# Rows of the second pair of sequences: turned by VectorE in squares of 32 and stored by SyncE, four tiles at a time

## Chip, cores and metric

The kernel runs on one core of a Trainium2 chip. The metric is the time of one execution on the device in microseconds (us). Engines are named as in the profile: PE is TensorE (PEld its weight loads), DVE VectorE, ACT ScalarE, POOL GpSimd, SP SyncE.

## What is computed

Sliding-window attention with a linear bias by distance for 8 sequences of 576 positions and 8 heads of 64, followed by a mixture of 8 experts in which each token goes to its best expert only.

```python
scores = q @ k.T / sqrt(64)                       # per sequence and head
scores = where(0 <= i - j < 128, scores - slope[h] * (i - j), -1e9)
attn = softmax(scores) @ v                        # (8, 8, 576, 64)
x = attn.transpose(0, 2, 1, 3).reshape(4608, 512)
logits = x @ w_gate                               # (4608, 8)
e = argmax(logits, 1); gate = softmax(logits)[e]
y[n] = gate[n] * (relu(x[n] @ w1[e[n]]) @ w2[e[n]])   # w1 512x1024, w2 1024x512
```

All of it is in float32.

## The kernel before

**Attention.** The sequences are taken in four pairs (bp = 0 to 3), the heads in four pairs (hp), which gives 16 units u = 4 bp + hp. A unit has four steps (g = 0 to 3), so the main loop runs over i = 4u + g, from 0 to 63. At each step `scores` are computed some three steps ahead (TensorE at L785, exponentials on ScalarE at L794 and L804, the factor of distance on VectorE at L798), `values` multiplies the probabilities with v into one accumulator (L828), and `finish` closes half a unit: ScalarE copies the accumulator into xT of the pair (L845, L847), TensorE adds up the probabilities (L859) and VectorE or ScalarE put the sums into sumT. There are two xT buffers, so that pair 2 writes into the buffer of pair 0, and pair 3 into that of pair 1. The accumulator `at` has one buffer, the small PSUM tile `m` two.

**Loads.** SyncE loads q, k and v of unit u + 2 during unit u. Each load follows a tiny transfer (`no_earlier_than`, L638) that reads a probability just made and so holds SyncE's queue to the pace of the loop. SyncE works through its queue in order.

**What is done with a finished pair.** `behind(bp)` gives a list of tasks; one is carried out at each step of the pair that follows. They compute the gate logits of the pair (`gate`, `turn`), the softmax scales `es` (`scale_a` to `scale_c`), each token's place (`count`, `place`, `ones_at`, `enlist`), and they write the pair's rows of x, with their scales, to `x_rows` in DRAM. A pair has nine tiles t of 128 rows; the ninth holds the last 64 rows of both sequences. The rows are written in one of two ways:

- *Turned by TensorE* (`row_turned`, `row_out`; pairs 1 and 2): four transposes of 128x128 into PSUM (L1067), a ScalarE copy to a row buffer `xs` (L1069), a POOL copy of the scales (L1076), one store of whole rows of 2,112 bytes by POOL (L1081).
- *Turned by VectorE* (`squares_turned`, `squares_scaled`, `squares_out`; pairs 0 and 3): VectorE transposes the tile in squares of 32 x 32 (L1118), POOL adds the scales brought into the same order (L1126; four small matmuls and two ScalarE copies in `scales_squared` make them once for each pair), and the stores put each square's rows of 528 bytes in their place (L1137): four stores for a tile, eight for the ninth. Pair 3 stores four tiles at a time by SyncE, out of a buffer of its own.

The row buffers come from the pool `rows`, which has four. They go round: a tile that asks for a buffer gets the one used four tiles earlier, and its writer waits until the stores out of it have landed.

**Order.** The order of instructions on each engine is that in which the program issues them (`manual_schedule`); waits for data and for buffers are added to it. After the attention the experts are computed, two after each other with a fast matrix multiplication of seven products. The rows of the first expert are gathered by POOL from `x_rows` of pairs 0 to 2 (L1271) before pair 3 is done; TensorE turns them (L1296) and the experts' matmuls follow.

Of the kernel before, what the change touches and what calls it, by code (L numbers as in the profile page):

```python
# [8 lines left out]
F32 = mybir.dt.float32  # L9
# [7 lines left out]
P = 128  # L17
# [441 lines left out]
def kernel(  # L459
# [12 lines left out]
    nc = tc.nc  # L472
# [12 lines left out]
    TPB = 2 * S // P  # L485
# [13 lines left out]
    NA = P // TQ  # L499
    PD = HP * TQ  # L500
    PW = PD + HP
# [5 lines left out]
    with ExitStack() as fast:  # L507
        def pool(stack, name, bufs, **kw):
            return stack.enter_context(tc.tile_pool(name=name, bufs=bufs, **kw))

        tail, att, late = ExitStack(), ExitStack(), ExitStack()
# [5 lines left out]
        ps_m = pool(fast, "ps_m", 2, space=PSUM)  # L517
        xp = pool(tail, "xp", 2, side="right")
        small = pool(tail, "small", 1, side="right")
        rows = pool(tail, "rows", 4, side="right")  # L520

# [185 lines left out]
        def placed(bp, t):  # L709

            b = 2 * bp * S
            if t < 8:
                return [(0, P, b + t // 4 * S + t % 4 * P)]
            return [(0, KB, b + 4 * P), (KB, KB, b + S + 4 * P)]
# [158 lines left out]
        def gate(bp, c):  # L873
            if bp not in gs:
                gs[bp] = xp.tile([P, 2 * S], F32, name="gs", bufs=1)
            ps = ps_m.tile([P, 512], F32, name="m")
            c0, n = ((0, LQ), (LQ, LQ), (2 * LQ, P))[c]
            for hp in range(HP):
                nc.tensor.matmul(
                    ps[32 * hp : 32 * hp + 32, :n], lhsT=wgd[:, hp, :], rhs=xT[bp][:, hp, c0 : c0 + n],  # L880
                    start=True, stop=True,
                )
            if c < 2:
                nc.vector.tensor_tensor(gs[bp][:, c0 : c0 + n], ps[:, :n], sumT[bp][:, :LQ], op=ALU.add)
            else:
                nc.vector.tensor_tensor(
                    gs[bp][:, c0 : c0 + n].rearrange("p (b q) -> p b q", b=2),
                    ps[:, :n].rearrange("p (b q) -> p b q", b=2),
                    sumT[bp][:, None, LQ:].to_broadcast([P, 2, S - LQ]), op=ALU.add,
                )  # L890
# [5 lines left out]
        def turn(bp, part):  # L896

            if part == 0:
                gsr[bp] = small.tile([P, TPB, P], F32, name="gsr")
            t0, n = ((0, 4), (4, 4), (8, 1))[part]  # L900
            ps = ps_m.tile([P, 512], F32, name="m")
            for k in range(n):
                nc.tensor.transpose(ps[:, k * P : (k + 1) * P], gs[bp][:, (t0 + k) * P : (t0 + k + 1) * P], ident[:])
            nc.scalar.copy(gsr[bp][:, t0 : t0 + n, :].rearrange("p t c -> p (t c)"), ps[:, : n * P])
# [155 lines left out]
            nc.vector.scalar_tensor_tensor(to, in0=sl(0), scalar=64.0, in1=sl(1), op0=ALU.mult, op1=ALU.add)  # L1060

        xs_of = {}

        def row_turned(bp, t):
            ps = ps_m.tile([P, 512], F32, name="m")
            for hp in range(HP):
                nc.tensor.transpose(ps[:, hp * P : (hp + 1) * P], xT[bp][:, hp, t * P : (t + 1) * P], ident[:])  # L1067
            xs = xs_of[bp, t] = rows.tile([P, NA, PW], F32, name="xs")
            nc.scalar.copy(  # L1069
                xs[:, :, :PD].rearrange("p a (h f) -> p h a f", h=HP), ps.rearrange("p (h a f) -> p h a f", h=HP, a=NA),  # L1070
            )
# [11 lines left out]
        def row(bp, t):  # L1083
            row_turned(bp, t)
            row_out(bp, t)
# [3 lines left out]
        spare = {}  # L1089
# [16 lines left out]
        def squares(bp, t):  # L1106
            if (bp, t) not in xs_of:
                if bp in spare and t < TPB - 1:
                    w = NA * PW
                    flat = spare[bp].rearrange("p h n -> p (h n)")  # L1110
                    xs_of[bp, t] = flat[:, t * w : (t + 1) * w].rearrange("p (k w) -> p k w", k=NA)
                else:
                    xs_of[bp, t] = rows.tile([P, NA, PW], F32, name="xs")
            return xs_of[bp, t]

        def squares_turned(bp, t):
            xs = squares(bp, t)
            nc.vector.transpose(  # L1118
                xs[:, :, :PD].rearrange("p k (h j) -> p k h j", h=HP),
                xT[bp][:, :, t * P : (t + 1) * P].rearrange("p h (k i) -> p k h i", k=NA),  # L1120
            )

        def squares_scaled(bp, t, n=1):

            for k in range(t, t + n):
                nc.gpsimd.tensor_copy(squares(bp, k)[:, :, PD:], sq_of[bp][:, k])  # L1126

        def squares_out(bp, t, eng, n=1):
            if n == 1:
                xs = xs_of.pop((bp, t))  # L1130
            else:
                w = NA * PW
                flat = spare[bp].rearrange("p h n -> p (h n)")
                xs = flat[:, t * w : (t + n) * w].rearrange("p (k w) -> p k w", k=n * NA)
            for p0, m, r0 in placed(bp, t):
                for a in range(NA):
                    eng.dma_start(  # L1137
                        x_d[r0 : r0 + n * m, a * PW : (a + 1) * PW].rearrange("(k i) w -> i k w", i=TQ),
                        xs[a * TQ : (a + 1) * TQ, p0 // TQ : p0 // TQ + n * m // TQ, :],
                    )  # L1140
# [120 lines left out]
        def gather(g, src):  # L1261
            nm = "" if g["n"] == NJ else "1"
            g["xg"] = g["pool"].tile([P, g["n"], NA, PW], F32, name="xg" + nm)
            for j in range(g["n"]):
                c = g["c0"] + j
                if in_rows(g):
                    todo = [(g["xg"][:, j].rearrange("p a w -> p (a w)"), src, g_idx[:, c : c + 1])]
                else:
                    todo = [(g["xg"][:, j, k, :], x_pieces, p_idx[:, c - NR * NJ, k : k + 1]) for k in range(NA)]
                for to, where, idx in todo:  # L1270
                    nc.gpsimd.indirect_dma_start(  # L1271
                        out=to, out_offset=None, in_=where, in_offset=bass.IndirectOffsetOnAxis(ap=idx, axis=0),
                    )
# [66 lines left out]
        def behind(bp):  # L1340

            g3 = [lambda k=k: gate(bp, k) for k in range(3)]
            t3 = [lambda k=k: turn(bp, k) for k in range(3)]
            rs = [lambda t=t: row(bp, t) for t in range(TPB)]
            a, a2, b, b2, c, n, q, p, p2, o, o2, e = (
                [lambda f=f: f(bp)] for f in (
                    scale_a, scale_a2, scale_b, scale_b2, scale_c, count, scales_squared, place, place2, ones_at,
                    ones_at2, enlist,
                )
            )  # L1350
            if bp == 0:
                rt = [lambda t=t: squares_turned(bp, t) for t in range(TPB)]
                ro = [
                    lambda t=t: (squares_scaled(bp, t), squares_out(bp, t, nc.gpsimd)) for t in range(TPB)
                ]
                return [g3[0:1], g3[1:2], g3[2:] + t3[0:1], t3[1:], a, a2 + rt[0:1], b + rt[1:2], b2 + rt[2:3],
                        c + n + rt[3:4], [], q + p, p2 + ro[0:4], o, o2, rt[4:6], e + rt[6:8] + ro[4:8]]
            rt, ro = ([lambda t=t, f=f: f(bp, t) for t in range(TPB)] for f in (row_turned, row_out))
            if bp == 1:
                last = [lambda: squares_turned(0, TPB - 1), lambda: squares_scaled(0, TPB - 1),  # L1360
                        lambda: squares_out(0, TPB - 1, nc.gpsimd)]
                return [g3[0:1] + last, g3[1:2], g3[2:] + t3[0:1], t3[1:], a + rt[0:1], a2 + rt[1:2], b + rt[2:3],
                        b2 + rt[3:4], c + n, [], p + ro[0:2], p2 + ro[2:4] + rs[4:5], o + rs[5:6], o2 + rs[6:7], rs[7:8], e + rs[8:9]]
            return [g3, t3, a + a2, b + b2 + rt[0:1], c + n + rt[1:2], rt[2:4], p + p2 + ro[0:4], o + o2 + rs[4:6],
                    rs[6:9] + [early_holes], e + [early_table, lambda: gather(fixed[0], x_d[: 3 * 2 * S, :])]]

        tasks = []
# [20 lines left out]
        for i in range(NG):  # L1388
            u, g = divmod(i, 4)
            bp, hp = units[u]  # L1390
# [34 lines left out]
            if g == 3 and hp == HP - 1 and bp < BP - 1:  # L1425
                tasks.extend(behind(bp))
# [318 lines left out]
```

## Time and profile before

| | us |
|---|---|
| median of 3 runs | 726.83 (726.69 to 732.29) |
| the profiled execution | 679.21 |
| its span, first to last instruction | 677.5 |
| PE busy | 649.8 (96%) |
| DVE busy | 363.9 (54%) |
| ACT busy | 217.0 (32%) |
| POOL busy | 240.3 (35%) |

The span is that of the profiled execution, from its first to its last instruction; the median is that of executions without a profile. Durations and times of day below are in microseconds from the start of the profiled span. In the lists of the profile a line begins with the line of the kernel and the engine; "idle before" is time in which the engine had nothing to run just before that instruction, with what ended it behind the arrow. The attention part takes the first 170 us or so, the experts the rest.

### The profile page before, as it was taken

The page shows a single profiled execution, that of the slowest core. Times are in us where ns is not written, and L with a number is a line of the kernel's source. Part 1 is how long each engine was busy: PE and PEld are TensorE (multiplying, and loading weights), DVE is VectorE, ACT ScalarE, POOL GpSimd, SP SyncE. Part 2 cuts the span into 40 slices and gives each one's busy share as a digit, 9 for nine tenths or more (in the row PEclk, how much of TensorE's full clock was granted, in tenths as well). Part 3 has the DMA queues.
Part 4 walks back from the last instruction along what each step waited for, and adds up shares of the span by engine and source line. Part 5 has one row for each costly group of instructions (what it writes and reads, how often), then busy time and mean ns, then how long its engine had stood idle before and what let it go on. Part 6 is the DMA issues. An engine that isn't in the chain of part 4 may idle for free.

```text
span 677.5 us, 14654 instructions
## 1 busy us (share of the span) xinstructions
PE 649.8 (96%) x6004; PEld 543.5 (80%) x6004; DVE 363.9 (54%) x727; ACT 217.0 (32%) x493; POOL 240.3 (35%) x372
## 2 busy tenths in 40 slices
PE   6899789999999999999999999999999999999995
PEld 5778668787788888978888887889788878878893
DVE  3346748776597768435642761484257426623510
ACT  6767547686331231023102311320231023113200
POOL 8000571325032572247026621732371256112020
PEclk9999989999999999999999999999999999999998
DMA  9887976964438944582376518444823674184010
GB/s 263 238 222 194 313 205 216 321 191 141 145 73 269 328 150 141 177 288 62 127 255 225 166 48 288 165 153 147 304 65 137 219 250 145 58 288 153 1 63 8
DMA packets 63166, 122.00 MB, mean 180 GB/s; under 512 B 5905, under 2 KB 29489, under 8 KB 63090
## 3 DMA queue, kind: packets, MB, share of 16 engines
q1 hardware_dynamic: 51138, 92.51, 42.8%
q0 software_dynamic: 10800, 27.58, 12.9%
q8 instruction: 49, 0.80, 0.5%
q10 hardware_dynamic: 1152, 0.88, 0.4%
q14 instruction: 27, 0.22, 0.1%
HBM read 101.79 MB, written 19.96 MB: 180 GB/s over the span
## 4 chain that ended last, share of the span: by engine, by line
PE 57%; issue 25%; POOL 10%; DMA 4%; DVE 2%; ACT 1%; POOLq 0%; DVEq 0%; ACTq 0%
PE pair1a L1552 4%; PE pair1b L1552 4%; PE pair0b L1495 4%; PE pair0a L1495 4%; PE pair0a L1552 4%; PE pair0b L1552 4%; PE pair2b L1495 4%; PE pair2a L1495 4%; POOL xg L1271 4%; DMA x_rows<-xs 3%; PE pair1b L1495 3%; PE pair1a L1495 3%; PE pair2a L1552 3%; PE pair2b L1552 3%; PE pair0a L1607 2%
## 5 line engine op out<-in xcount | busy, mean ns | idle before, releaser
L1271 POOL DMA_INDIRECT xg<-x_rows,p_idx x124 | 125.4, 1011 | 37.8 <-issue 37.5
L1575 POOL DMA_INDIRECT out_dram<-zo,s_idx x39 | 44.5, 1140 | 244.5 <-DVE zo L1566 142.8
L798 DVE TENSOR_TENSOR pe<-pe,fac 128x512 f32<-128x512 f32 x64 | 43.8, 687 | 45.7 <-ACT pe L794 44.9
L785 PE MATMUL sp<-q_sb,k_sb 64*64 64x192 f32 (+2 forms) x1152 | 58.9, 324 | 6.9 <-DMA q_sb<-in_qT_dram 5.4
L828 PE MATMUL at<-pe,v_sb 64*64 64x192 f32 (+2 forms) x1408 | 58.5, 286 | 3.3 <-issue 3.3
L785 PEld LDWEIGHTS sp<-q_sb,k_sb 64*64 64x64 f32 x1152 | 41.4, 138 | 16.1 <-DMA q_sb<-in_qT_dram 4.4
L828 PEld LDWEIGHTS at<-pe,v_sb 64*64 64x64 f32 x1408 | 47.0, 135 | 9.0 <-issue 6.4
L794 ACT ACTIVATE pe<-sp 128x512 f32<-128x512 f32 x64 | 38.2, 598 | 37.9 <-issue 15.9
L804 ACT ACTIVATE pe<-sp,mid 128x128 f32<-128x128 f32 x128 | 39.7, 366 | 0.0
L1506 ACT ACTIVATE h<-h 128x512 f32<-128x512 f32 x32 | 20.2, 631 | 38.6 <-DVE h L1505 38.6
L859 PE MATMUL m<-pe,ind 128*32 128x192 f32 (+2 forms) x704 | 29.7, 286 | 2.7 <-issue 2.7
L1137 POOL DMA_DIRECT2D x_rows<-xs x48 | 26.0, 549 | 9.5 <-DMA x_rows<-xs 4.6
L1283 DVE TENSOR_TENSOR xn<-xg 128x512 f32<-128x512 f32 x39 | 26.3, 677 | 3.5 <-DMA xg<-x_rows,g_idx 3.0
L859 PEld LDWEIGHTS m<-pe,ind 128*32 128x32 f32 x704 | 23.2, 109 | 5.1 <-issue 3.1
L1299 DVE STREAM_TRANSPOSE xgT<-xn 128x512 f32<-128x512 f32 x31 | 22.0, 711 | 1.1
L538 DVE TENSOR_TENSOR w2s<-w 128x512 f32<-128x512 f32 x16 | 10.9, 684 | 20.8 <-DMA w<-in_moe_w_dram 20.8
L1607 PE MATMUL pair2a<-w,h 128*128 128x512 f32 x48 | 21.1, 592 | 0.0
L1126 POOL COPY xs<-sq 128x16 f32<-128x16 f32 x10 | 2.4, 242 | 52.6 <-ACT sq L1104 52.6
L845 ACT COPY xT<-at 128x640 f32<-128x640 f32 (+1 forms) x32 | 19.0, 594 | 4.5 <-PE at L828 2.6
L1495 PE MATMUL pair0a<-xgT,w 128*128 128x256 f32 x72 | 17.1, 380 | 0.7 <-ACT xgT L1297 0.7
L1495 PE MATMUL pair0b<-xgT,w 128*128 128x256 f32 x72 | 17.2, 382 | 0.0
L1552 PE MATMUL pair1a<-w,h 128*128 128x256 f32 x72 | 17.1, 380 | 0.0
(378 smaller groups left out, 1385.0 us busy)
## 6 DMA issues: line engine op xcount, KB each, us to landing
w<-in_moe_w_dram SPq DMA_DIRECT2D x29, 2048.0 KB, 7.9
k_sb<-in_kT_dram SPq DMA_DIRECT2D x15, 576.0 KB, 5.6
q_sb<-in_qT_dram SPq DMA_DIRECT2D x15, 576.0 KB, 6.3
v_sb<-in_v_dram SPq DMA_DIRECT2D x30, 288.0 KB, 4.9
x_rows<-xs POOLq DMA_DIRECT2D x16, 264.0 KB, 4.7
x_rows<-xs POOLq DMA_DIRECT2D x32, 66.0 KB, 5.7
x_rows<-xT SPq DMA_DIRECT2D x8, 264.0 KB, 5.8
w<-in_moe_w_dram SPq DMA_DIRECT2D x4, 512.0 KB, 8.2
```

The lines of the kernel that those rows point to most:

```text
L785: nc.tensor.matmul(by_distance(sp[c * KB : (c + 1) * KB, r, :GC], kb, 0, n), lhsT=k_sb[u][hs, c, kb * KB : (kb + 1) * KB], rhs=q_sb[u][hs, ...
L794: nc.scalar.activation(outer, sp[:, :, :GC].rearrange("p r (j x) -> p r j x", j=3)[:, :, 0:3:2, :], AF.Exp, scale=SCALE,)
L798: nc.vector.tensor_tensor(outer, outer, fac[:, h0 : h0 + 2, : 2 * w].rearrange("p r (j x) -> p r j x", j=2)[:, :, :, : 2 * KB], op=ALU.mult,)
L804: nc.scalar.activation(pe[:, r, inner], sp[:, r, inner], AF.Exp, bias=mid[:, h0 + r : h0 + r + 1], scale=SCALE,)
L828: nc.tensor.matmul(acc[r * D : (r + 1) * D, c, lo - q0 : hi - q0].rearrange("p (j x) -> p j x", x=KB), lhsT=v_sb[u][c * KB : (c + 1) * KB, ...
L859: nc.tensor.matmul(sm[32 * j : 32 * j + 32, lo - q0 : hi - q0].rearrange("p (j x) -> p j x", x=KB), lhsT=none[:] if pe is None else ind[:, ...
L1271: nc.gpsimd.indirect_dma_start(out=to, out_offset=None, in_=where, in_offset=bass.IndirectOffsetOnAxis(ap=idx, axis=0),)
L1283: nc.vector.tensor_tensor(xn[:], x, s.unsqueeze(3).to_broadcast([P, NA, HP, TQ]), op=ALU.mult)
L1495: nc.tensor.matmul(ps[:, f * 256 : (f + 1) * 256], lhsT=left[m][:, d, fb * P : (fb + 1) * P], rhs=right[m][:, d, :], start=(m in (1, 2, 5) ...
L1552: nc.tensor.matmul(ps[:, :256], lhsT=left[m][:, f, c * P : (c + 1) * P], rhs=right[m][:, f, :], start=(m in (1, 2, 5) and f == 0), stop=Tr ...
L1575: ins = nc.gpsimd.indirect_dma_start(out=out[:, :], out_offset=bass.IndirectOffsetOnAxis(ap=s_idx[:, g["c0"] + j : g["c0"] + j + 1], axis= ...
L1607: nc.tensor.matmul(ps[:], lhsT=g["h"][:, fb, :], rhs=g["w2"][:, fb, :], start=(fb == 0), stop=(fb == FB - 1),)
```

## The change

Pair 1 is now turned by VectorE as pair 0 is, and its first eight tiles are stored by SyncE in two batches of four tiles (four stores of 32 x 16 x 132 numbers for each batch). The four row buffers become one tile `rows4` with four slots: tile t uses slot t mod 4, but the ninth tile (t = 8) uses slot 3. That holds for pairs 0, 1 and 2, and for pair 3's ninth tile. Pair 1's ninth tile is turned and stored one pair later, in the second task of pair 2's list, as pair 0's already was in the first task of pair 1's. `scales_squared` is added for pair 1.

```diff
--- before.py
+++ after.py
@@ -517,7 +517,7 @@
         ps_m = pool(fast, "ps_m", 2, space=PSUM)
         xp = pool(tail, "xp", 2, side="right")
         small = pool(tail, "small", 1, side="right")
-        rows = pool(tail, "rows", 4, side="right")
+        rows = pool(tail, "rows", 1, side="right")
 
 
 
@@ -1060,12 +1060,16 @@
             nc.vector.scalar_tensor_tensor(to, in0=sl(0), scalar=64.0, in1=sl(1), op0=ALU.mult, op1=ALU.add)
 
         xs_of = {}
+        rows4 = rows.tile([P, 4, NA, PW], F32, name="rows4")
+
+        def slot_of_row(t):
+            return rows4[:, 3 if t == TPB - 1 else t % 4]
 
         def row_turned(bp, t):
             ps = ps_m.tile([P, 512], F32, name="m")
             for hp in range(HP):
                 nc.tensor.transpose(ps[:, hp * P : (hp + 1) * P], xT[bp][:, hp, t * P : (t + 1) * P], ident[:])
-            xs = xs_of[bp, t] = rows.tile([P, NA, PW], F32, name="xs")
+            xs = xs_of[bp, t] = slot_of_row(t)
             nc.scalar.copy(
                 xs[:, :, :PD].rearrange("p a (h f) -> p h a f", h=HP), ps.rearrange("p (h a f) -> p h a f", h=HP, a=NA),
             )
@@ -1110,7 +1114,7 @@
                     flat = spare[bp].rearrange("p h n -> p (h n)")
                     xs_of[bp, t] = flat[:, t * w : (t + 1) * w].rearrange("p (k w) -> p k w", k=NA)
                 else:
-                    xs_of[bp, t] = rows.tile([P, NA, PW], F32, name="xs")
+                    xs_of[bp, t] = slot_of_row(t)
             return xs_of[bp, t]
 
         def squares_turned(bp, t):
@@ -1129,9 +1133,12 @@
             if n == 1:
                 xs = xs_of.pop((bp, t))
             else:
-                w = NA * PW
-                flat = spare[bp].rearrange("p h n -> p (h n)")
-                xs = flat[:, t * w : (t + n) * w].rearrange("p (k w) -> p k w", k=n * NA)
+                if bp in spare:
+                    w = NA * PW
+                    flat = spare[bp].rearrange("p h n -> p (h n)")
+                    xs = flat[:, t * w : (t + n) * w].rearrange("p (k w) -> p k w", k=n * NA)
+                else:
+                    xs = rows4[:].rearrange("p s k w -> p (s k) w")
             for p0, m, r0 in placed(bp, t):
                 for a in range(NA):
                     eng.dma_start(
@@ -1359,9 +1366,15 @@
             if bp == 1:
                 last = [lambda: squares_turned(0, TPB - 1), lambda: squares_scaled(0, TPB - 1),
                         lambda: squares_out(0, TPB - 1, nc.gpsimd)]
+                rt = [lambda t=t: squares_turned(bp, t) for t in range(TPB)]
+                scaled = [[lambda t=t: squares_scaled(bp, t, 4)] for t in (0, 4)]
+                ro = [[lambda t=t: squares_out(bp, t, nc.sync, 4)] for t in (0, 4)]
                 return [g3[0:1] + last, g3[1:2], g3[2:] + t3[0:1], t3[1:], a + rt[0:1], a2 + rt[1:2], b + rt[2:3],
-                        b2 + rt[3:4], c + n, [], p + ro[0:2], p2 + ro[2:4] + rs[4:5], o + rs[5:6], o2 + rs[6:7], rs[7:8], e + rs[8:9]]
-            return [g3, t3, a + a2, b + b2 + rt[0:1], c + n + rt[1:2], rt[2:4], p + p2 + ro[0:4], o + o2 + rs[4:6],
+                        b2 + rt[3:4], c + n, [], q + p + scaled[0], p2 + ro[0], o, o2, rt[4:6],
+                        e + rt[6:8] + scaled[1] + ro[1]]
+            last = [lambda: squares_turned(1, TPB - 1), lambda: squares_scaled(1, TPB - 1),
+                    lambda: squares_out(1, TPB - 1, nc.gpsimd)]
+            return [g3, t3 + last, a + a2, b + b2 + rt[0:1], c + n + rt[1:2], rt[2:4], p + p2 + ro[0:4], o + o2 + rs[4:6],
                     rs[6:9] + [early_holes], e + [early_table, lambda: gather(fixed[0], x_d[: 3 * 2 * S, :])]]
 
         tasks = []
```

## Prediction

> **What bounds the kernel now.** I read the page first, then the busy time by stretches, then the timelines of TensorE, VectorE, ScalarE and POOL where the change acts. One profiled execution took 679.21 us, its span 677.5.
>
> ```profile
> PE 649.8 (96%) x6004; PEld 543.5 (80%) x6004; DVE 363.9 (54%) x727; ACT 217.0 (32%) x493; POOL 240.3 (35%) x372
> ...
> PE   6899789999999999999999999999999999999995
> ...
> DVE  3346748776597768435642761484257426623510
> ```
>
> TensorE is the bound almost everywhere; slices 3 to 5 (51 to 102 us, where pair 0's rows are stored) are its weakest after the start. What is taken from TensorE can be gained, what makes it wait is lost. By groups of instructions the work in question costs:
>
> ```profile
> L1067 PE MATMUL m<-ident,xT 128*128 128x128 f32 x72 | 11.3, 285 | 0.9 <-DVE sumT L870 0.5 <-ACT xs L1069 0.4
> ...
> L1069 ACT COPY xs<-m 128x512 f32<-128x512 f32 x18 | 10.4, 586 | 5.2 <-PE m L1067 3.2 <-issue 0.9 <-DMA x_rows<-xs 0.7
> ...
> L1118 DVE STREAM_TRANSPOSE xs<-xT 128x512 f32<-128x512 f32 x10 | 7.0, 701 | 5.1 <-DMA x_rows<-xs 4.1 <-POOL xs L1126 1.0
> ```
>
> The last row matters most: VectorE already waits for stores before it may overwrite a row buffer. Busy time by stretches (columns: TensorE, weight loads, VectorE, ScalarE, POOL, then granted clock, DMA share, GB/s):
>
> ```profile
> 86.00:89.30 3.30, 3.30 (x50) 2.23 (x51) 1.57 (x4) 1.11 (x3) 1.82 (x4) 0.52 0.91 270
> ...
> 102.00:114.00 12.00, 12.00 (x290) 10.15 (x286) 9.75 (x29) 9.94 (x26) 0.00 (x0) 1.00 0.71 223
> 114.00:132.00 18.00, 17.10 (x403) 14.34 (x393) 15.28 (x36) 12.40 (x31) 8.03 (x18) 1.00 0.93 299
> ```
>
> In pair 1's stretch VectorE works 25.0 of 30 us, and most of its rest is the gap between dependent short operations: in 102 to 130 us it waits only 0.6, 0.5 and 0.6 us for others. It has little room for transposes.
>
> Now the place where pair 0's last tile (t=8) is turned, in the timelines of POOL, VectorE, ScalarE and TensorE, and the store latency of t=7:
>
> ```profile
> 87.83 1.09 POOL L1137 DMA_DIRECT2D x_rows<-xs  x2 [1.31 <-DMA x_rows<-xs]
> ...
> 95.07 2.17 POOL L1137 DMA_DIRECT2D x_rows<-xs  x4 [0.29 <-POOL xs L1126]
> ```
>
> ```profile
> 90.36 0.69 DVE L884 TENSOR_TENSOR gs<-m,sumT 128x512 f32<-128x512 f32 x1
> 93.44 0.71 DVE L1118 STREAM_TRANSPOSE xs<-xT 128x512 f32<-128x512 f32 x1 [2.39 <-DMA x_rows<-xs]
> ```
>
> ```profile
> 94.24 0.69 ACT L845 COPY xT<-at 128x640 f32<-128x640 f32 x1 [1.92 <-DVE xs L1118]
> ```
>
> ```profile
> 95.38 0.43 PE L879 MATMUL m<-xT,wgd 128*32 128x128 f32 x8 [1.58 <-DVE gs L884]
> ```
>
> ```profile
> L1137 POOL DMA_DIRECT2D x_rows<-xs x4: 548/548/548, 95.1 to 96.7; - x4
> ...
> DMA to landing us min/median/max: 2.4/2.9/3.5
> ```
>
> With four rotating buffers t=8 takes the buffer of t=4, whose last stores go out at 87.83 and 88.38; VectorE waits 2.39 us for them. ScalarE's copy into pair 2's xT (the buffer pair 0's xT leaves) waits for that transpose, and TensorE waits 1.58 us behind it.
>
> [...] all of ScalarE stood 1.92 us behind one transpose. [...] Here the clock was 0.52 in 86.0 to 89.3, after an idle stretch at 82.9 to 85.0: 3.3 x 0.48 = 1.6 us lost. [...] the squares are put in place by the store; the trace has 0.70 us for 128x512. [...] the last pair's SyncE stores in 528-byte pieces ran at 196 GB/s with a DMA share of 0.85 (197.0 to 209.5), pair 1's stretch above at 299 with 0.93.
>
> **The change part by part.** The built program's order gives the places; a step i is a quarter of a unit.
>
> 1. *TensorE and ScalarE freed.* Four transposes hold TensorE 0.59 us (119.02 to 119.61), so nine tiles 5.3 us. Four matmuls for the squared scales come in: pair 0's took 1.0 us (69.21). Net -4.3 us. ScalarE loses 9 x 0.59 and gains 2 x 0.27.
>
> 2. *VectorE loaded.* Nine transposes at 0.63 spacing (61.48 to 62.11) are 5.7 us. Four stand before pair 1's es (114.34): 2.5 us, less the two waits of 0.6 and 0.5 that they fill, so es is 1.4 later, at 116.0. TensorE would arrive there at 112.2 (114.53 less 4 x 0.59) without its four transposes; but the new matmuls need es and are queued ahead of the scores. They end at 117.0, where before the next matmul began at 114.94: +2.0 instead of a gain. Four more transposes (t=4 to 7) push VectorE to 134.0 at the end of step 47 (130.1 before), less its 2.06 us of waiting before 132.16. TensorE needs its gs for the third gate matmul and comes out +1.35 behind, having spent its other transposes on waiting.
>
> 3. *Pair 0's t=8, the largest part.* It now shares slot 3 with t=7, the tile just before it. Its transpose waits for t=7's four stores: the last issued at 96.71, landing 2.4 to 3.5 later, 99.1 to 100.2. It starts near 99.7 instead of 93.44: +6.3 on VectorE, on the ScalarE copy behind, on TensorE, which has nothing else queued. The idle stretch grows to about 8 us[...]: +1.6 as above (bounds 0 and 3.2).
>
> 4. *Pair 1's t=8* is now the last reader of xT of pair 1, in slot 3 behind the second SyncE batch. The batch is issued when t=7 is turned, 134.0. At the 196 GB/s above 1.08 MB take 5.5 us, and about 1.1 pass before data flow: landed 140.6, turned 141.3. Behind it wait ScalarE's copy of unit 12 into that xT (137.64 before) and TensorE's next values, which need the accumulator that the copy frees: 142.1 against 139.11+1.35. So +1.65; pair 1 in all +3.0 (bounds -4.3, all of the saving, and +6).
>
> 5. *SyncE's queue.* Eight stores stand ahead of loads, 0.3 to 1.8 us each (median 0.92). The first four put unit 13's k and q about 4 us later; they are used at 134.29, 14 us after q's issue: covered. The second four hold unit 14's k (128.41) until about 138, q until 139.3, landed near 144; its scores come at 144.62+3.0. Cover 3.6 us, nothing charged; without it its overrun counts. POOL loses ten stores of 0.55 and gets eight for t=8: not on the path.
>
> 6. *Pair 2's t=8* also shares slot 3 with t=7, and here ScalarE does the writing:
>
> ```profile
> 158.29 0.54 POOL L1081 DMA_DIRECT2D x_rows<-xs  x1 [0.30 <-POOL xs L1076]
> ```
>
> ```profile
> 157.32 0.58 ACT L1069 COPY xs<-m 128x512 f32<-128x512 f32 x1 [0.39 <-PE m L1067]
> ```
>
> ```profile
> 159.42 0.25 PE L859 MATMUL m<-fac,none 128*32 128x64 f32 x2
> ...
> 168.07 0.63 PE L1296 MATMUL m<-ident,xn 128*128 128x128 f32 x4 [1.08 <-DVE xn L1283]
> ```
>
> That t=7 store landed 3.9 us after issue, at 162.2. The copy moves from 157.32 to 162.2; TensorE's sums at 159.42 need the PSUM buffer it frees: 162.9, +3.5. Its own stores leave 4.0 later, the first gather waits for them, and TensorE already waited 1.08 us for the gathered rows: +4.0 in all (bounds 2.6 and 5).
>
> Sum: 6.3 + 1.6 + 3.0 + 4.0 = +14.9. Everything after about 170 us is TensorE back to back and only moves. 679.2 becomes 694.1. The runs shown have a median of 726.83, 47.6 above the profiled one; the profile does not say where that lies. I add the same 14.9: 741.7.
>
> **Rivals.** (a) *The slots do not bite and TensorE's saving comes through.* One mechanism: VectorE and ScalarE reach the shared slot after its stores have landed. For pair 0 VectorE would have to come at 99.7 and not 91.05. Then -4.3: 722.5, not slower. For it: unprofiled runs are longer, so engines may come later against the stores. Against it: the t=7 stores follow from POOL's own issue, 0.55 us each. (b) *VectorE is no bound, only the slots count*: point 2 gives the saving back, 6.3 + 1.6 - 4.3 + 4.0 = 7.6, and with a milder second stall 5: 732. (c) *Every stall drops the clock* (points 2, 4, 6 also), and unit 14's loads come late by 2: 14.9 + 4.8 + 2 = 21.7: 748.5. That the change does not take place is excluded by the built order.
>
> **How the numbers follow.** Chances: forecast 0.62, (a) 0.08, (b) 0.18, (c) 0.12. About 1% (7.3 us) is what a measurement of this kernel can tell from no change. Slower by more: the forecast, (c) and a quarter of (b), 0.78. Within it: the rest of (b) and some of (a), 0.17. Faster by more: 0.05. The range leaves out (a) and the upper end of (c): with 5.9, no clock loss, -4.3 and 2.6 the low end is +4, 731; the high end is that of (c): 730 to 750.
>
> **What would show it.** VectorE's wait before pair 0's t=8 near 9 us instead of 2.39, TensorE idle about 8 us there with a low clock after it; TensorE waiting for es near step 42; VectorE waiting for the SyncE stores before pair 1's t=8; ScalarE waiting about 5 us for a store before pair 2's t=8. I am wrong if those waits are under 2 us each, or if the attention part ends no later than before.

## The result, and the profile after

| | before | after |
|---|---|---|
| median, first series | 726.76 (4 runs) | 748.41 (747.03 to 749.95) |
| median, repeated later | 681.72 (34 runs) | 699.87 (698.16 to 704.24) |
| profiled execution, first series | 679.21 | 749.50 |

The changed kernel is slower: ratio 1.0278, 95% interval 1.0228 to 1.0327, +21.65 us; in the later series 1.0273 (1.0220 to 1.0325), +18.15 us. The forecast was 741.7, with 730 to 750 as its range.

The spans of the two first profiles may not be subtracted. The level of all kernels differs by about 46 us between series, before included (726.8 and 729.1 in two, 682.7 and 681.7 in two others; the last three series ran on three different chips), and the first profile of before fell on the low level; experiment 1 shows that most of this lies in the expert part. So I compare ratios, and in the traces the times at which TensorE begins each unit's first sums (L859, tile `m` from `fac,none`, at step g = 2 of the unit), and the moment at which it turns the first expert's first rows (L1296 before, L1303 after; 168.07 before, 190.72 after). From there to the end, before took 509.4 us and after, profiled at the same level, 508.9 (699.4 - 190.5). The whole loss is in the attention part. Up to that moment the changed kernel lost 22.65 us against the first profile of before (190.72 - 168.07) and 16.4 against the second (174.31), so two profiles of one kernel differ there by 6.2. This table has the stretches, in us:

| from first sums of unit | 8 to 9 | 9 to 10 | 10 to 11 | 11 to 12 | 12 to 13 | 13 to 14 | 14 to first rows turned |
|---|---|---|---|---|---|---|---|
| before | 12.31 | 8.42 | 10.32 | 13.63 | 9.84 | 12.07 | 8.65 |
| before, second profile | 15.19 | 8.42 | 10.33 | 14.03 | 9.85 | 12.07 | 11.24 |
| after | 21.01 | 7.77 | 15.09 | 14.82 | 14.94 | 14.01 | 9.55 |
| after, second profile | 20.50 | 7.77 | 15.28 | 14.82 | 14.89 | 14.01 | 10.03 |

Against the first profile of before: pair 0's ninth tile +8.7, the stretch of `es` +4.8 and +1.2 behind it, pair 1's ninth tile +5.1, pair 2's +1.9 and +0.9 behind it, less 0.65 saved from 9 to 10. Now the page of after, its part with busy times and slices (a slice is 18.7 us here, not 17):

```profile
PE 672.8 (90%) x5976; PEld 554.2 (74%) x5976; DVE 367.0 (49%) x736; ACT 210.0 (28%) x486; POOL 236.7 (32%) x370
...
PE   6888858878899967999899989979998999799996
...
DVE  3437618856498636613562284237335622743500
...
PEclk9999968999999987999899999998998999999999
```

TensorE has a hole in slice 5 (94 to 112 us), VectorE is nearly idle in it, and the granted clock drops there to 0.6. The busy totals belong to profiles at different levels and don't measure the change. The groups of instructions:

```profile
L1071 PE MATMUL m<-ident,xT 128*128 128x128 f32 x36 | 5.4, 284 | 0.3 <-ACT rows L1073 0.3
```

```profile
L1073 ACT COPY rows<-m 128x512 f32<-128x512 f32 x9 | 5.1, 588 | 4.5 <-DMA x_rows<-rows 3.9 <-ACT xT L847 0.4
```

```profile
L1122 DVE STREAM_TRANSPOSE rows<-xT 128x512 f32<-128x512 f32 x19 | 13.1, 699 | 17.5 <-DMA x_rows<-rows 17.4
```

Half the TensorE transposes are gone, as intended; VectorE's nine more cost 6.1 us of work. The number that counts is in the last column: VectorE stood 17.4 us ahead of transposes until stores had landed, against 4.1 before. Busy time by stretches (TensorE, weight loads, VectorE, ScalarE, POOL, the clock granted to TensorE with 1.00 for full speed, DMA share, GB/s):

```profile
90.00:100.00 10.00, 3.48 (x72) 2.07 (x68) 2.44 (x4) 1.11 (x3) 8.03 (x17) 0.78 0.82 239
100.00:110.00 10.00, 6.33 (x95) 4.79 (x95) 2.87 (x5) 3.20 (x7) 4.62 (x10) 0.54 0.31 72
...
120.00:130.00 10.00, 6.61 (x104) 5.71 (x100) 8.48 (x25) 3.51 (x10) 0.61 (x4) 0.82 0.57 164
130.00:140.00 10.00, 10.00 (x254) 8.82 (x251) 7.45 (x18) 6.29 (x17) 1.54 (x4) 0.84 0.92 240
...
150.00:160.00 10.00, 6.26 (x113) 4.78 (x108) 4.41 (x13) 4.35 (x11) 2.96 (x7) 0.85 0.99 245
```

Each low clock falls into or behind a wait of TensorE. The first wait, at pair 0's ninth tile, in the timelines of VectorE, ScalarE and TensorE:

```profile
101.80 0.71 DVE L1122 STREAM_TRANSPOSE rows<-xT 128x512 f32<-128x512 f32 x1 [8.32 <-DMA x_rows<-rows]
...
103.00 0.68 DVE L884 TENSOR_TENSOR gs<-m,sumT 128x512 f32<-128x512 f32 x1
```

```profile
102.60 0.69 ACT L845 COPY xT<-at 128x640 f32<-128x640 f32 x1 [10.67 <-DVE rows L1122]
```

```profile
103.67 0.65 PE L879 MATMUL m<-xT,wgd 128*32 128x128 f32 x8 [9.17 <-ACT sumT L868]
...
114.54 0.25 PE L859 MATMUL m<-fac,none 128*32 128x64 f32 x2
```

It is the chain of before with 8.32 us in place of 2.39 at its head. The profile names ScalarE's copy as the releaser, but VectorE's `gs` (103.00 + 0.68) ends in the same moment and frees the PSUM buffer that the gate matmul writes; in before `gs` is the one named, and in experiment 4 the gate matmul starts before that copy. TensorE waits for VectorE here. The second and third wait, both in pair 1's work, on TensorE, VectorE and SyncE's queue:

```profile
126.43 1.96 PE L1100 MATMUL m<-es,to_squares 128*128 128x72 f32 x8 [3.16 <-DVE es L975]
...
157.50 1.56 PE L828 MATMUL at<-pe,v_sb 64*64 64x64 f32 x24 [3.50 <-ACT xT L845]
```

```profile
155.96 0.71 DVE L1122 STREAM_TRANSPOSE rows<-xT 128x512 f32<-128x512 f32 x1 [4.64 <-DMA x_rows<-rows]
```

```profile
147.48 3.44 SPq L1144 DMA_DIRECT2D x_rows<-rows  x4
```

SyncE issues the second batch in 3.44 us from 147.48 on, and its slots are free at 155.96, 8.5 us after the first issue. The last wait, pair 2's ninth tile, on ScalarE and TensorE:

```profile
180.54 0.59 ACT L1073 COPY rows<-m 128x512 f32<-128x512 f32 x1 [3.87 <-DMA x_rows<-rows]
```

```profile
181.17 0.25 PE L859 MATMUL m<-fac,none 128*32 128x64 f32 x2 [1.95 <-ACT rows L1073]
```

So every wait of the forecast is there. The question for the experiments is what each is worth, and why 21.65 and not 14.9.

### The profile page after: what moved, and what is told of

The parts are those of the page before. It is cut to its first block, busy times and chain, and to the rows that moved or that the text cites. A ratio compares the mean times of both kernels' runs of the same rounds, so it can differ in the third digit from the quotient of the medians.

```text
span 747.8 us, 14607 instructions
## 1 busy us (share of the span) xinstructions
PE 672.8 (90%) x5976; PEld 554.2 (74%) x5976; DVE 367.0 (49%) x736; ACT 210.0 (28%) x486; POOL 236.7 (32%) x370
## 4 chain that ended last, share of the span: by engine, by line
PE 67%; issue 11%; another core or an unknown queue 6%; DVE 6%; DMA 4%; ACT 3%; POOL 2%; SPq 0%; ACTq 0%; DVEq 0%; POOLq 0%
PE pair1b L1565 4%; PE pair1a L1565 4%; PE sp L785 4%; PE pair0a L1508 4%; PE pair0a L1565 4%; PE pair0b L1508 4%; PE at L828 4%; PE pair2a L1508 4%; PE pair2a L1565 4%; PE pair0b L1565 3%; PE pair2b L1508 3%; PE pair2b L1565 3%; PE pair1a L1508 3%; PE pair1b L1508 3%
## 5 line engine op out<-in xcount | busy, mean ns | idle before, releaser
L785 PE MATMUL sp<-q_sb,k_sb 64*64 64x192 f32 (+2 forms) x1152 | 61.7, 334 | 8.1 <-DMA q_sb<-in_qT_dram 5.2
L828 PE MATMUL at<-pe,v_sb 64*64 64x192 f32 (+2 forms) x1408 | 60.4, 291 | 8.1 <-ACT xT L845 4.5
L828 PEld LDWEIGHTS at<-pe,v_sb 64*64 64x64 f32 x1408 | 48.7, 140 | 15.2 <-issue 6.1
L785 PEld LDWEIGHTS sp<-q_sb,k_sb 64*64 64x64 f32 x1152 | 42.8, 142 | 17.6 <-issue 6.1
L1130 POOL COPY rows<-sq 128x16 f32<-128x16 f32 x19 | 4.8, 272 | 103.2 <-ACT sq L1108 76.9
L1144 POOL DMA_DIRECT2D x_rows<-rows x56 | 30.3, 549 | 12.0 <-DVE pe L798 3.4
L859 PE MATMUL m<-pe,ind 128*32 128x192 f32 (+2 forms) x704 | 30.8, 286 | 3.5 <-issue 3.4
L859 PEld LDWEIGHTS m<-pe,ind 128*32 128x32 f32 x704 | 23.2, 109 | 6.9 <-issue 4.9
L1565 PE MATMUL pair1b<-w,h 128*128 128x256 f32 x72 | 21.2, 423 | 4.8 <-issue 4.8
L1565 PE MATMUL pair0a<-w,h 128*128 128x256 f32 x64 | 18.5, 440 | 3.9 <-ACT h L1537 3.9
L1122 DVE STREAM_TRANSPOSE rows<-xT 128x512 f32<-128x512 f32 x19 | 13.1, 699 | 17.5 <-DMA x_rows<-rows 17.4
L1565 PEld LDWEIGHTS pair1b<-w,h 128*128 128x128 f32 x72 | 14.8, 210 | 8.8 <-issue 6.8
```

Of the source, the lines that this page charges most:

```text
L785: nc.tensor.matmul(by_distance(sp[c * KB : (c + 1) * KB, r, :GC], kb, 0, n), lhsT=k_sb[u][hs, c, kb * KB : (kb + 1) * KB], rhs=q_sb[u][hs, ...
L828: nc.tensor.matmul(acc[r * D : (r + 1) * D, c, lo - q0 : hi - q0].rearrange("p (j x) -> p j x", x=KB), lhsT=v_sb[u][c * KB : (c + 1) * KB, ...
L859: nc.tensor.matmul(sm[32 * j : 32 * j + 32, lo - q0 : hi - q0].rearrange("p (j x) -> p j x", x=KB), lhsT=none[:] if pe is None else ind[:, ...
L1144: eng.dma_start(x_d[r0 : r0 + n * m, a * PW : (a + 1) * PW].rearrange("(k i) w -> i k w", i=TQ), xs[a * TQ : (a + 1) * TQ, p0 // TQ : p0 / ...
L1565: nc.tensor.matmul(ps[:, :256], lhsT=left[m][:, f, c * P : (c + 1) * P], rhs=right[m][:, f, :], start=(m in (1, 2, 5) and f == 0), stop=Tr ...
```

## Experiments

Two theories, called S and V in the expectations (L and Q where the stretch of `es` is split further). S: the row buffer that the ninth tile shares with the eighth, and the low clock behind its wait, are most of the loss. V or L: VectorE's nine added transposes are. Q: the four matmuls for the squared scales stand too early in TensorE's queue.

### 1. The kernel before, profiled again (control_before)

No edit.

> The kernel before, unchanged, profiled a second time. Theory A (all of the loss lies in the attention part): in this trace the expert part, from the first expert matmul to the end, also takes 540 to 560 us, with waits of about 7 us, as in the profile of the changed kernel (551.8), while the rows of the first expert are transposed near 168 us as in the first profile of before. Theory B (the change lengthens the expert part as well): the expert part takes about 505 us again.

Span 728.9, first expert rows turned at 174.31: the rest took 554.6 us, as in the changed kernel's first profile (747.8 - 190.72 = 557.1). The waits in it are the same ones; the longest of TensorE there, before (second profile) and after:

```profile
266.98 3.78 PE L1495 MATMUL pair1a<-xgT,ws 128*128 128x256 f32 x8 [10.63 <-DVE h L1517]
```

```profile
284.48 3.78 PE L1508 MATMUL pair1a<-xgT,ws 128*128 128x256 f32 x8 [10.66 <-DVE h L1530]
```

Theory A holds: the expert part's level has nothing to do with the change. What sets that level was not studied. The first rows were turned at 174.31 and not near 168, as expected: 2.9 of these 6 us lie between units 8 and 9, and 2.6 behind unit 14.

### 2. A buffer of its own for the ninth tile (own_slot)

The table `seen_i` is not used after the start, so its place serves as fifth row buffer for pairs 0 to 2.

```diff
+        row5 = ac.tile([P, NA, PW], F32, name="seen_i")
-        def slot_of_row(t):
-            return rows4[:, 3 if t == TPB - 1 else t % 4]
+        def slot_of_row(bp, t):
+            if t == TPB - 1:
+                return rows4[:, 3] if bp == BP - 1 else row5
+            return rows4[:, t % 4]
```

> The changed kernel, with a fifth row buffer for the ninth tile of pairs 0, 1 and 2. Theory S (the shared buffer and the low clock after its wait are most of the loss): from the lags at the units' first sums it takes back 8.7 us at pair 0's ninth tile, some 4.5 at pair 1's and 2 at pair 2's, so about 733 us, +6 over before; VectorE waits under 1 us ahead of each ninth tile. Theory V (VectorE's load is the bound, and time gained at pair 0 is lost again behind VectorE in pair 1): at most 4 us come back, 744 us or more.

Ratio 1.0007 (0.9984 to 1.0031): the whole loss comes back, more than S asked for, and V falls as an explanation of the +21.65. Unit 8 to 9 takes 10.06 us, less than in either profile of before, because before waited at this place as well. The wait is gone from VectorE's timeline:

```profile
90.83 0.71 DVE L1125 STREAM_TRANSPOSE rows<-xT 128x512 f32<-128x512 f32 x1 [1.00 <-DMA x_rows<-rows]
92.64 0.70 DVE L1125 STREAM_TRANSPOSE seen_i<-xT 128x512 f32<-128x512 f32 x1
```

But 10 to 11 still takes 15.75 us and 11 to 12 14.81: part of the change's cost remains and is paid out of what the free buffer gains at pair 0.

### 3. The shared buffer alone (before_shared)

The kernel before with four fixed slots; pair 1's ninth tile keeps away from the eighth tile's slot.

```diff
+            return rows4[:, 3 if t == TPB - 1 and bp != 1 else t % 4]
```

> The kernel before, with nothing changed but the buffer of the ninth tile of pairs 0 and 2, which is the eighth tile's. Theory S: +8.7 us at pair 0 (wait of VectorE about 8, clock near half for 10 us after it) and +2 to 4 at pair 2: about 738 us. Theory V: pair 0's stall is taken up by the slack behind it, at most +3, 730 us.

Ratio 1.0193 (1.0165 to 1.0222), +12.6 us by the medians (741.66 against 729.09); S said 738. Three stretches are longer than in both profiles of before: 8 to 9 with 21.39, 13 to 14 with 16.34 (12.07), and from 14 to the first rows with 13.21 (8.65 and 11.24). VectorE and ScalarE at the two places:

```profile
101.31 0.71 DVE L1122 STREAM_TRANSPOSE rows<-xT 128x512 f32<-128x512 f32 x1 [8.03 <-DMA x_rows<-rows]
```

```profile
172.64 0.59 ACT L1073 COPY rows<-m 128x512 f32<-128x512 f32 x1 [6.20 <-DMA x_rows<-rows]
```

The buffer rule, without any of the rest of the change, makes a slowdown of about two thirds of the size by the ratios.

### 4. The clock behind the wait (after_fill, after_fill25)

In the changed kernel, matmuls that nobody reads, into unused columns of the sums' PSUM tile, fill TensorE's idle stretch; 34 and then 25 of them.

```diff
+            if (u, half) == (8, 0):
+                for k in range(25):
+                    nc.tensor.matmul(sm[:, 320:512], lhsT=ident[:], rhs=fac[:, 0, 0:192], ...)
```

> The changed kernel, with 34 matmuls of 192 columns that nobody reads ahead of TensorE's wait behind pair 0's ninth tile, about 7.5 us of them in an idle stretch of 9. If the low clock after the idle stretch is a cost of its own: clock near 1 in 92 to 110 us instead of 0.78 and 0.54, and 4 to 5 us come back, about 744 us. If the clock doesn't matter, because VectorE, ScalarE and the stores set the pace there: no difference, 748 us.

Ratio 1.0291 (1.0263 to 1.0319), no gain, although the clock was 1.00 from 90 to 110 us (sixteen matmuls of L785 took 0.88 us at 105.00, and 1.56 at 105.30 in after). I had taken 0.22 us for one such matmul; TensorE's timeline (two records for each of the 34), and VectorE's below it, show that it takes 0.333:

```profile
92.58 11.32 PE L868 MATMUL m<-fac,ident 128*128 128x192 f32 x68
103.83 0.43 PE L885 MATMUL m<-xT,wgd 128*32 128x128 f32 x8
```

```profile
100.95 0.68 DVE L890 TENSOR_TENSOR gs<-m,sumT 128x512 f32<-128x512 f32 x1
```

VectorE's `gs`, which the gate matmul (now L885) waits for, had ended at 101.63: the filler itself was late by 2.2 us. (The expectation that follows says 2.6, counted from ScalarE's copy of xT.) With 25:

> The changed kernel with 25 instead of 34 matmuls ahead of TensorE's wait behind pair 0's ninth tile. 34 took 11.32 us, 0.333 each, and ended 2.6 us after the copy that TensorE waited for; 25 take 8.3 us and end before it. If the clock after the idle stretch is a cost of its own: 2.6 us less than with 34, unit 8's first sums to unit 9's in about 18 us instead of 21, ratio to before 1.025. If not: 1.028 as with the change alone.

Ratio 1.0243 (1.0190 to 1.0297). Unit 8 to 9 takes 17.72 us in place of 21.01 and 20.50. Part of this is a shorter wait (VectorE stood 7.41 us for the stores, and 8.32 and 7.75 in the two profiles of after). The clock shows in what comes behind it, from the gate matmul to unit 9's first sums:

```profile
103.38 0.43 PE L885 MATMUL m<-xT,wgd 128*32 128x128 f32 x8
...
111.80 0.25 PE L859 MATMUL m<-fac,none 128*32 128x64 f32 x2
```

These are 8.42 us, and 8.49 with 34 matmuls, where the two profiles of after have 10.87 and 10.93 for the same instructions: the low clock is worth about 2.5 us here. The times alone don't settle it, as the interval overlaps that of the change (1.0220 to 1.0325), and in this profile 13 to 14 took 15.47, 1.5 more than in after.

### 5. Place by place (after_again, own_p0, own_p01)

The changed kernel, and then the fifth buffer for pair 0 alone, and for pairs 0 and 1.

```diff
-                return rows4[:, 3] if bp == BP - 1 else row5
+                return rows4[:, 3] if bp > 0 else row5        # own_p0; bp > 1 in own_p01
```

> The changed kernel unchanged, beside the next three on the same chip. +21 us over before, as first measured (+21.65).

> The changed kernel with the fifth row buffer for pair 0's ninth tile alone; pairs 1 and 2 share the eighth tile's. Theory S: the shares of the three places add up. In the traces unit 9's first sums came 9.4 us late with the change and 2.3 us early with all three buffers free, on the clock of the first profile of before, so about 11 of the 21 come back: +10 us, ratio 1.014. If the pairs behind take most of it back (VectorE late again, then SyncE's batch): +15 or more.

> The same with the fifth buffer for the ninth tiles of pairs 0 and 1. Theory S: pair 1's tile no longer waits for SyncE's second batch, and unit 12's first sums to unit 13's take 11.5 us instead of 14.9: 3.5 to 5 us less than with pair 0's alone, +5 to +6 us, ratio 1.008; the rest, 2 to 4 us at pair 2, comes back with the third (1.0007 measured).

Ratios 1.0273 (1.0220 to 1.0325), 1.0082 (1.0051 to 1.0112) and 1.0060 (1.0035 to 1.0085): +18.15, +5.8 and +3.9 us (medians 699.87, 687.48, 685.60). Pair 0 gives back 12.4 of 18.15, more than the 11 I had expected; the expectation for the total, +10, missed by 4. (after_again itself came out at +18.15 and not +21, on a lower level and at the same ratio.) Pair 0's stretch is 9.40 us in place of 20.50. Between own_p0 and own_p01 the times overlap: 1.9 us by the medians, where I had expected 3.5 to 5. But in the trace 12 to 13 falls from 14.91 to 10.93, and with own_slot 13 to 14 falls from 14.01 to 12.35. So in these traces the three shared slots are worth about 11, 4 and 2 us of TensorE's time. The first is the least certain: in the six profiles of the changed kernel's variants where pair 0's slot is free, its stretch takes 9.40 to 12.70 us.

In own_p01 a smaller wait comes to light in 12 to 13, in TensorE's timeline and SyncE's:

```profile
147.93 0.88 PE L785 MATMUL sp<-q_sb,k_sb 64*64 64x192 f32 x16 [1.06 <-DMA q_sb<-in_qT_dram]
```

```profile
134.94 3.44 SPq L1147 DMA_DIRECT2D x_rows<-rows  x4
...
140.84 0.38 SPq L597 DMA_DIRECT2D q_sb<-in_qT_dram  x1
```

The load of unit 14's q stands behind the batch and goes out at 140.84; in before with a fifth buffer (experiment 7) it went out at 130.09. With the shared slot the longer wait covers this one.

### 6. What is left in pair 1: the squared scales or VectorE (q_later, no_turns, late_turns)

All three start from the fifth buffer for all pairs. q_later puts the four matmuls for the squared scales one step later:

```diff
-                        b2 + rt[3:4], c + n, [], q + p + scaled[0], p2 + ro[0], o, o2, rt[4:6],
+                        b2 + rt[3:4], c + n, [], p, p2 + q + scaled[0] + ro[0], o, o2, rt[4:6],
```

> The changed kernel with a fifth row buffer, and pair 1's matmuls for the squared scales (with POOL's scales behind them) one step later, about 2.4 us. Theory Q: the wait for es and the clock lost behind it (2.96 us, and about 2.8 us at 0.81 and 0.84 for 20 us) go: about 5 us less than with the fifth buffer alone, ratio to before 0.994. Theory L: VectorE is the bound of this stretch, its later results come when they came, and TensorE waits at the next gate matmul instead: ratio 1.000 as with the fifth buffer alone.

Ratio 1.0036 (1.0017 to 1.0056): Q falls. TensorE now waits for the next result of VectorE, and longer later:

```profile
117.37 0.36 PE L990 MATMUL m<-pre,lt_strict 128*128 128x8 f32 x2 [3.18 <-DVE pre L981]
...
138.24 3.73 PE L879 MATMUL m<-xT,wgd 128*32 128x512 f32 x24 [4.59 <-DVE sumT L870]
```

no_turns leaves out VectorE's transposes of pair 1's first eight tiles, so their stored rows are old ones:

```diff
-                rt = [lambda t=t: squares_turned(bp, t) for t in range(TPB)]
+                rt = [lambda: None for t in range(TPB)]
```

> The changed kernel with a fifth row buffer for the ninth tile, and VectorE's eight transposes of pair 1's tiles 0 to 7 left out: old rows are stored. With the fifth buffer alone the time was that of before (ratio 1.0007) although TensorE has lost 4.3 us of work: unit 10's first sums to unit 11's took 15.75 us instead of 10.33. Theory L (VectorE's added 5 us make es late): the wait for es falls from 2.96 us to under 1 and unit 10 to 11 takes about 10.5 us; ratio to before 0.991, about 6 us less. Theory Q (the four matmuls for the squared scales stand in TensorE's queue before es can be there, whatever VectorE's load): the wait stays above 2 us, ratio 0.998 or more.

Ratio 0.9941 (0.9917 to 0.9965). L said 0.991, a wait under 1 us and 10.5 us for 10 to 11; the wait is 1.00 and the stretch takes 10.97, so L holds, with less gain in the time.

```profile
111.17 1.08 PE L1103 MATMUL m<-es,to_squares 128*128 128x72 f32 x8 [1.00 <-DVE es L975]
```

The eight transposes cost 7.8 us of the stretch from unit 9 to 14 (54.32 without, 62.15 with them). late_turns keeps them but puts the first four behind `es`:

```diff
-                ... t3[1:], a + rt[0:1], a2 + rt[1:2], b + rt[2:3],
-                        b2 + rt[3:4], c + n, [], q + p + scaled[0], p2 + ro[0], o, o2, rt[4:6],
+                ... t3[1:], a, a2, b,
+                        b2, c + n, rt[0:2], q + p + rt[2:4] + scaled[0], p2 + ro[0], o, o2, rt[4:6],
```

> The fifth buffer for all three, and pair 1's first four transposes moved behind es in VectorE's order (two at the step after it, two at the next), where VectorE waited 1.18, 1.27, 0.38 and 0.42 us for ScalarE in the trace of the fifth buffer alone. Theory L: es comes 2.5 us earlier, TensorE's wait for it falls from 2.96 us to under 1, its clock stays at 1.00, and 3 to 4 us come back: ratio 0.995. If VectorE's work as a whole is the bound from 100 to 140 us, the wait turns up later, at sumT and gs (1.91 and 0.62 before): ratio 1.000.

Ratio 0.9963 (0.9943 to 0.9983): 0.4% faster than before. The wait for `es` falls from 2.96 to 0.99, 10 to 11 takes 12.25 in place of 15.75, and 11 to 12 stays at 14.80, where the last four transposes still stand. The clock did not stay at 1.00, as I had expected: it was 0.83 in 110 to 120 us (sixteen matmuls of L785 took 1.56 us at 116.95).

```profile
114.41 1.08 PE L1103 MATMUL m<-es,to_squares 128*128 128x72 f32 x8 [0.99 <-DVE es L975]
```

### 7. The free buffer without the change (before_own)

The kernel before with the fifth buffer alone (and fixed slots, as in experiment 3).

> The kernel before with the fifth row buffer for the ninth tile of pairs 0 to 2 and nothing else. If the wait of VectorE for the stores of pair 0's fifth tile (2.39 and 2.17 us in two profiles of before) is on the path, with TensorE's wait behind it (1.58 and 3.08): 3 to 4 us less than before, ratio 0.995. If the slack behind it takes it up: ratio 1.000.

Ratio 0.9954 (0.9932 to 0.9975), about 3.1 us less, as expected if that wait is on the path (3.9 us by the medians, 678.78 against 682.67); 8 to 9 takes 10.91 in place of 12.31 and 15.19. It beats both kernels. late_turns (0.9963) can't be told from it: with the waits mended, turning pair 1 by VectorE is worth nothing that these runs show, for or against.

## Why the prediction was right in sign and short by 6.7 us

Place by place, against the first profile of before, pair 0 cost 8.7 us where 7.9 was forecast, pair 1 10.4 (-0.65 + 4.8 + 1.2 + 5.1) where 3.0 was, and pair 2 2.8 where 4.0 was. So pair 1 is what the forecast was short of.

**Step 3, pair 0's ninth tile: right in mechanism, short in both terms.** Forecast +6.3 and +1.6; measured +8.7 against the first profile of before (+5.8 against the second, which had lost more there itself), and this with two of the nine transposes gone from the stretch, 1.2 us. From unit 8's first sums to the gate matmul TensorE took 10.14 us and not 2.55: +7.6 for the wait (7.6 + 2.5 - 1.2 = 8.9, an estimate, against the 8.7). VectorE started at 101.80 against 99.7, since POOL issued t=7's stores from 98.00 on and not from 95.07. The clock cost about 2.5 us (experiment 4), and not the 1.6 that I had carried over, as an estimate, from a shorter idle stretch (82.9 to 85.0). After this wait of 9.17 us sixteen matmuls of L785 took 1.56 us at 105.30 and 1.48 at 107.92, and only from 109.19 on do the lines have the lengths of full clock (24 matmuls of L828 in 0.86 us, 1.50 at 106.63): 5.5 us after work began again at 103.67. Behind the wait of 3.50 us that ends at 157.50 it took about 3 us, behind that of 3.16 at 126.43 over 6. Waits of about 2 us were enough for a drop in some cases (last section).

**Step 2, VectorE's load: the wait was right, what follows from it was not priced.** I had `es` 3.8 us behind TensorE's arrival; the wait was 3.16. But I charged +2.0 at these matmuls with the clock at 1.00, and unit 10 to 11 lost 4.8, of which 0.65 had been saved just before: +4.1. The clock was 0.82 and 0.84 for the next 20 us. TensorE's busy time times what is missing of the clock is 6.61 x 0.18 + 10.00 x 0.16 = 2.8 us, an estimate, and somewhat more than the 2.1 that are missing; no run tested the clock here. At "+1.35 behind" for the end of step 47 the sum stood at +5.3 (units 9 to 12). What is shown is the size of VectorE's eight transposes as a whole: 7.8 us (experiment 6).

**Step 1, what TensorE is freed of: most of it did not arrive.** The 4.3 us were saved as work: TensorE did 5.4 us of transposes and not 11.3. Two of the nine stood between units 8 and 9 (counted under step 3), the other seven, 4.1 us, between 9 and 12. Of these 0.65 us came through, from 9 to 10; the rest did not become time. Even in no_turns, without VectorE's load, units 9 to 14 take 54.32 us, against 54.28 in before. TensorE waits there 1.00, 0.63, 0.68, 0.24, 0.94 and 0.28 us where before waited 0.41, 0.49, 0.24 and 0.37: 2.3 us of new waits, and 1.08 of new matmuls, out of 4.1 us of transposes; the other 0.7 us I can't name. no_turns gains its 0.6% at pair 0, where before_own gains 0.46% without leaving out any work. That the first line of the page shows TensorE as the bound did not make its work worth its length.

**Step 4, pair 1's ninth tile: right chain, term too small.** Forecast +1.65, measured +5.1. I had the batch landed 6.6 us after t=7 was turned; it took 8.5 (147.42 to 155.96). 3.44 us of that are SyncE's issue of four stores, about 0.86 each, which I had not counted apart from the rate. The clock behind it was 0.85: 6.26 x 0.15 = 0.9 us more, an estimate. Experiment 5 shows 4.0 of the 5.1 to hang on the shared slot.

**Step 5, SyncE's queue: the cover was too short.** I charged nothing for unit 14's loads. In own_p01 TensorE waits 1.06 us for that q, 1.60 in own_slot: in own_p01 the load went out at 140.84, where I had 139.3, and the wait for it ended at 147.93, where I had its data near 144. In the change itself the wait of step 4 hides it, so nothing was missed in the sum, but the reason given was wrong.

**Step 6, pair 2's ninth tile: right, too large.** TensorE waited 1.95 and not 3.5; the stretch 13 to 14 lost 1.9 and the whole rest 2.8, against +4.0. (The second profile of before took 2.6 us longer behind unit 14 by itself, so the last 0.9 are uncertain.)

**The rivals.** (a), that the slots don't bite, and (b), that VectorE is no bound, are excluded by experiments 2, 3 and 6. (c) came to 748.5, and 748.41 was measured; that it is so near is luck in part. Its mechanism, a drop of the clock behind every stall, is what the windows show at steps 2 and 4 (0.82 to 0.85), and at step 6 in the second profile of after only; but its late loads stayed hidden, and the rest of its sum is the forecast's. With busy time times missing clock over 90 to 170 us the changed kernel lost 7.6 us, before 1.4 (80 to 90 us): 6.2 more, an estimate, where I had charged 1.6. It is on the high side: at pair 0 (90 to 110 us) it gives 3.7, and experiment 4 shows 2.5. By these windows the clock, and the batch of step 4, are what the forecast was short of; step 6 went the other way. Only the 2.5 us at pair 0 are shown by an experiment; the rest of the clock's share is read from the windows. The kernel's level made no difference to the argument: I carried the sum over as it was, and the ratios of the two series agree.

## What to carry to other kernels

A rotating buffer is part of the schedule: before merging or renumbering slots, find for each writer the last store out of its slot and when it lands, since one tile that follows its slot's user at once can cost more than all that the change saves (12.4 us at pair 0, against 4.3 us of TensorE's work). When an engine whose order the program fixes is handed more work, place the work behind the result that another engine waits for (late_turns against own_slot: same work, 3.5 us of a stretch). And price a stall of TensorE with its clock (about 2.5 us behind the 9.17 here), and work taken from a busy engine at nothing until it is clear that the engines feeding it keep up (0.65 of 4.1 us here).

## What the hardware showed that I had not expected

- The clock fell behind some waits of TensorE of about 2 us. In after, from 30 to 240 us, windows of 1 us with a granted clock of 0.50 came in the wait of 9.17 us and behind those of 3.16 and 3.50 us; behind waits of 1.50, 1.58, 1.70 and 1.95 us it stayed at 1.00. In before 1.98 us of idle time, up to 85.02, were enough for the 0.52 that the prediction read, and 1.58 us at 95.38 were not. In seven other profiles (before_shared, after_fill, after_fill25, own_p0, own_p01, q_later, late_turns), from 80 to 200 us, the lengths of lines show it: the first sixteen matmuls of L785, which take 0.88 us at full clock, took 1.41 to 1.56 us behind 14 waits of 2.31 to 8.88 us, and behind a wait of 4.59 us (q_later) 24 matmuls of L879 took 3.73 us that took 2.31 in before (132.05). After 1.89 to 1.96 us it went both ways: they took 1.56 us behind 1.89 in own_p0 (80.07) and 1.95 in own_p01 (164.63), and 0.88 behind 1.92 in own_p0 (134.13) and 1.91 in late_turns (133.38). So it did even for one and the same wait: pair 2's ninth tile in the two profiles of after, first and second.

```profile
181.17 0.25 PE L859 MATMUL m<-fac,none 128*32 128x64 f32 x2 [1.95 <-ACT rows L1073]
...
180.00:190.00 10.00, 8.40 (x212) 6.91 (x212) 4.85 (x15) 6.07 (x16) 4.18 (x6) 1.00 0.25 59
```

```profile
180.47 0.32 PE L859 MATMUL m<-fac,none 128*32 128x64 f32 x2 [1.96 <-ACT rows L1073]
...
180.00:190.00 10.00, 9.15 (x216) 7.83 (x216) 5.19 (x15) 6.59 (x17) 4.70 (x6) 0.83 0.33 86
```

- Two short waits close together were followed by a low clock in one trace and not in another. In late_turns 0.99 and 0.70 us, ending at 114.41 and 116.20, came ahead of sixteen matmuls of L785 that took 1.56 us at 116.95; in no_turns 1.00 and 0.63 us came ahead of the same in 0.88 us at 113.43.
- A SyncE store of one batch (264 KB in pieces of 528 bytes) held SyncE's queue for about 0.86 us on the mean (3.44 for four, at 134.94 in own_p01), whereas loads of q and k took 0.38 and 0.46 in the same queue (at 140.84 and 139.36).
